# Gated sum of two linear-attention branches on one core: the key-value burst moved behind the first denominators, W' among later queries, 1/den by Ln and Exp

## The chip, the cores and the metric

The kernel runs on one core of one Trainium2 chip. The metric is the device time of one execution in microseconds (us). All executions used below ran in the fast state (granted TensorE clock 1.0), with one exception that is named where it comes up. PE is TensorE (PEld is its weight loads), DVE is VectorE, ACT is ScalarE, POOL is GpSimd, SP is SyncE. PSUM is the memory that the matmuls write to; in this kernel a PSUM bank stays taken until another engine has read it out (a *drain*). The experiments ran in three sets on three chips, each set with the kernel before in the same rounds, so across sets the ratios to it are compared and not the times.

## The reference, cut to what matters

```python
# two branches X in (A, B), each with its own wqkv and wo; S = 2048, D = 640, 32 heads of 20
qkv = x @ wqkv
phi = lambda t: jnp.where(t > 0, t + 1, jnp.exp(t)) + 1e-6
pq, pk = phi(q), phi(k)
kv  = einsum("bhsd,bhse->bhde", pk, v)
z   = einsum("bhsd->bhd", pk)
num = einsum("bhqd,bhde->bhqe", pq, kv)
den = einsum("bhqd,bhd->bhq", pq, z) + 1e-6
o   = (num / den) @ wo
out = g * o_A + (1 - g) * o_B        # g = sigmoid(sum(x * gate_w))
```

The kernel never forms `v`. For each branch it forms G = phi(k)ᵀx, then per head kv = G·Wv, and then W' = kv·Wo, so that the output is (phi(q)/den)·W'.

## The kernel before

A small list scheduler in the kernel's Python orders all operations. Each operation has a *planned* duration, and the scheduler also hands out the eight PSUM banks. The order and the banks are then fixed in the program.

The phases on PE are: keys of both branches, G of A, G of B, queries in four blocks of 512 rows (each block has five "query units" per branch), then the totals (`final`), 128 rows at a time. The key-value step `m_unit` (110 small matmuls for both branches, over two column groups of the array), its masks on DVE and the W' pairs sit at different places for the two branches. The small matmuls and the denominators are *column-tiled*: they use 64 and 32 columns of PE's array (`128*64` and `128*32` in the traces).

```python
def m_unit(X):                                   # 55 small matmuls into one bank, then three masks
    ...
    for q0, q1, g, w in ((0, 5, 0, 12), (0, 5, 1, 12), (5, 6, last, 8)):
        def mask(e, ...):
            return e.tensor_tensor(
                out=MB[p0 : p0 + n, q0:q1, 60 * g : 60 * g + n].rearrange("p q (i k) -> p q k i", k=NC),
                in0=PS[p0 : p0 + n, tile.banks[0], ...].rearrange("p (q k i) -> p q k i", k=NC, i=w),
                in1=m.unsqueeze(1).to_broadcast([n, q1 - q0, NC, w]), op=ALU.mult)
        sch.op("DVE", mask, _dve_ns(n * (q1 - q0)), ...)      # planned: 380 ns for 60x300

g_unit("B", 0); g_unit("B", 1); m_unit("A")      # A: inside the G phase of B
g_unit("B", 2)
for q in (0, 1): wp_unit("A", q)                 # W' pair: 2 matmuls into a pair of banks, one drain
...
queries(0)
m_unit("B")                                      # B: between query blocks 0 and 1,
queries(1)                                       #    W' pairs of B among the queries of block 1
wp_store("B"); wp_rows("B")                      # W' through DRAM, back as WPB
d01 = dens(0)                                    # denominators of blocks 0 and 1
scale_q(0, d01, 2)                               # ACT copies den, DVE reciprocal, factors through DRAM,
queries(2); queries(3)                           #    then DVE multiplies the queries
...
# ---- scale_q (cut) ----
e.activation(DN, PS[den], ACT.Identity, bias=EP)            # ACT
e.reciprocal(RC, DN)                                        # DVE
# ---- final (cut): for each piece of columns: A total, ACT drain times g; B total, DVE blend ----
```

## Time and profile before

| | before |
|---|---|
| time, median of the first 6 executions | 190.67 us (190.61 to 190.99) |
| span of the profiled execution | 189.5 us |
| PE / DVE / ACT busy | 98% / 68% / 40% |
| PE waiting, all at the start | 1.4 us |
| first query matmul | 94.98 us |

The first two parts of the page give the busy time of each engine and, below, its busy tenths in 40 slices of the span. The fourth part gives the chain of work that ended last; a q behind an engine's name is its queue or sequencer, and "issue" is time in which nothing visible was waited for.

```profile
PE 185.9 (98%) x1289; PEld 124.0 (65%) x1289; DVE 129.8 (68%) x275; ACT 76.5 (40%) x129; POOL 8.2 (4%) x14
...
PE   7999999999999999999999999999999999999995
...
DVE  1398998999600009996179997898999959933324
...
PE 94%; DMA 3%; SPq 1%; issue 0%; ACT 0%; DVE 0%; DVEq 0%; ACTq 0%
```

PE has no gap after its start, and the chain is PE for 94% of the span. Nothing that other engines do counts until it makes PE wait.

The groups by shape show busy us, mean ns of one instruction, and the idle time of the engine before them:

```profile
L793 DVE RECIPROCAL RC<-DN 128x256 bf16<-128x256 f32 x4 | 7.0, 1746 | 0.1
L647 DVE TENSOR_TENSOR MB<-ps,CB 60x300 bf16<-60x300 f32 x4 | 4.1, 1032 | 0.1
L787 ACT ACTIVATE DN<-ps,EP 128x256 f32<-128x256 f32 x4 | 1.9, 474 | 1.2 <-PE ps L383 1.1
```

The timeline (start us, duration us, what) of the small bursts and of the end:

```profile
105.86 1.13 PE L383 MATMUL ps<-GTB,WVB 128*64 128x60 bf16 x55
106.92 3.43 PE L383 MATMUL ps<-XT,WQA 128*128 128x512 bf16 x15
...
116.97 0.44 PE L383 MATMUL ps<-WOB,MB 124*120 124x320 bf16 x2
117.24 2.32 PE L383 MATMUL ps<-XT,WQB 128*128 128x512 bf16 x10
119.40 2.32 PE L383 MATMUL ps<-XT,WQA 128*128 128x512 bf16 x10
...
122.53 0.38 PE L383 MATMUL ps<-FE,ZBDB 128*32 128x512 bf16 x2
122.85 3.44 PE L383 MATMUL ps<-XT,WQA 128*128 128x512 bf16 x15
...
186.75 0.51 PE L383 MATMUL ps<-WPB,FE 128*128 128x160 bf16 x5
...
187.01 0.39 ACT L859 ACTIVATE TS<-ps,GA 128x160 f32<-128x160 f32 x1 [0.36 <-PE ps L383]
187.51 0.38 DVE L865 SCALAR_TENSOR_TENSOR OL<-ps,GA,TS 128x160 bf16<-128x160 f32 x1 [0.37 <-ACT TS L859]
```

Query matmuls start 0.216 us apart. After the denominators the next one comes 0.32 us later, so leaving a column-tiled burst costs 0.1 us. PE's last matmul ends at 187.26 (186.75 + 0.51), and the last blend at 187.89 (187.51 + 0.38).

### The profile page before, as it was taken

What the parts mean: (1) busy time and instruction counts of PE and PEld (TensorE: products, weight loads), DVE (VectorE), ACT (ScalarE), POOL (GpSimd) and SP (SyncE); (2) the same over time, 40 slices, a digit from 0 to 9 for tenths busy, and PEclk for the clock granted to TensorE, in tenths of its full rate; (3) what the DMA queues carried; (4) which work ended last, traced back from release to release, by engine and by line L of the source; (5) the groups of instructions that cost most, each with busy time, mean ns of one, the idle gap of its engine ahead of it and who ended that gap; (6) DMA issues with size and microseconds to landing.
All of it is one profiled execution on the core that took longest, in us unless ns stands there. A gap on an engine that the chain in (4) does not pass through costs nothing.

```text
span 189.5 us, 3208 instructions
## 1 busy us (share of the span) xinstructions
PE 185.9 (98%) x1289; PEld 124.0 (65%) x1289; DVE 129.8 (68%) x275; ACT 76.5 (40%) x129; POOL 8.2 (4%) x14
## 2 busy tenths in 40 slices
PE   7999999999999999999999999999999999999995
PEld 2555555555788888888855666455556677777774
DVE  1398998999600009996179997898999959933324
ACT  2265656565311122103255478565553422332232
POOL 8900000000000000000000000000000000000000
DMA  5999699991011111112143004675000173221212
GB/s 189 298 243 177 211 388 364 337 231 33 0 35 38 35 35 38 35 35 38 35 95 102 5 22 173 166 224 170 0 0 3 44 226 92 86 89 35 73 69 69
DMA packets 31936, 21.49 MB, mean 113 GB/s; under 512 B 16818, under 2 KB 31666, under 8 KB 31922
## 3 DMA queue, kind: packets, MB, share of 16 engines
q1 hardware_dynamic: 31490, 20.80, 39.5%
q10 hardware_dynamic: 432, 0.49, 0.8%
q8 instruction: 10, 0.16, 0.4%
q14 instruction: 4, 0.03, 0.1%
HBM read 12.05 MB, written 5.31 MB: 92 GB/s over the span
## 4 chain that ended last, share of the span: by engine, by line
PE 94%; DMA 3%; SPq 1%; issue 0%; ACT 0%; DVE 0%; DVEq 0%; ACTq 0%
PE ps L383 94%; DMA WK<-in_B_wqkv_dram 3%; SPq L372 1%; ACT TS L859 0%; DVE OL L865 0%; DVEq L276 0%; ACTq L276 0%
## 5 line engine op out<-in xcount | busy, mean ns | idle before, releaser
L383 PE MATMUL ps<-WK,XT 128*128 128x512 bf16 (+2 forms) x250 | 44.0, 337 | 0.5 <-DMA WK<-in_A_wqkv_dram 0.2
L383 PE MATMUL ps<-XN,FE 128*128 128x320 bf16 x320 | 44.3, 300 | 0.0
L383 PEld LDWEIGHTS ps<-XN,FE 128*128 128x128 bf16 x320 | 37.5, 118 | 5.9
L383 PEld LDWEIGHTS ps<-WK,XT 128*128 128x128 bf16 x250 | 24.1, 98 | 20.0 <-DMA WK<-in_A_wqkv_dram 0.5
L743 ACT ACTIVATE EK<-ps 128x512 bf16<-128x512 f32 x40 | 23.9, 597 | 18.5 <-PE ps L383 16.9
L563 ACT ACTIVATE EK<-ps 128x512 bf16<-128x512 f32 (+1 forms) x42 | 21.4, 526 | 16.2 <-PE ps L383 16.2
L752 DVE SCALAR_TENSOR_TENSOR FE<-ps,EK 128x512 bf16<-128x512 f32 x40 | 26.8, 688 | 0.7
L859 ACT ACTIVATE TS<-ps,GA 128x640 f32<-128x640 f32 (+2 forms) x18 | 13.2, 734 | 29.5 <-PE ps L383 29.5
L383 PE MATMUL ps<-WPB,FE 128*128 128x320 bf16 (+1 forms) x165 | 24.7, 295 | 0.0
L383 PE MATMUL ps<-WPA,FE 128*128 128x320 bf16 (+1 forms) x165 | 24.7, 295 | 0.0
L573 DVE SCALAR_TENSOR_TENSOR FE<-ps,EK 128x512 bf16<-128x512 f32 (+1 forms) x42 | 23.9, 596 | 0.5
L865 DVE SCALAR_TENSOR_TENSOR OS<-ps,GA,TS 128x640 bf16<-128x640 f32 x15 | 13.0, 869 | 14.7 <-PE ps L383 14.7
L383 PE MATMUL ps<-XT,WQA 128*128 128x512 bf16 x100 | 22.8, 380 | 0.0
L383 PE MATMUL ps<-XT,WQB 128*128 128x512 bf16 x100 | 22.7, 379 | 0.0
L600 ACT ACTIVATE GS<-ps 128x640 bf16<-128x640 f32 x10 | 7.0, 704 | 37.0 <-PE ps L383 37.0
L383 PEld LDWEIGHTS ps<-WPA,FE 128*128 128x128 bf16 x165 | 15.9, 98 | 6.1
L383 PEld LDWEIGHTS ps<-WPB,FE 128*128 128x128 bf16 x165 | 15.8, 98 | 6.2 <-ACT TS L859 0.4
L383 PEld LDWEIGHTS ps<-XT,WQB 128*128 128x128 bf16 x100 | 11.7, 117 | 9.1
L383 PEld LDWEIGHTS ps<-XT,WQA 128*128 128x128 bf16 x100 | 11.6, 118 | 9.4 <-issue 0.4
L705 DVE SCALAR_TENSOR_TENSOR GP<-XN,GWB 128x640 bf16<-128x640 bf16 x16 | 13.3, 829 | 4.1 <-PE ps L383 3.6
L811 DVE TENSOR_TENSOR FE<-FE,RX 128x1280 bf16<-128x1280 bf16 (+1 forms) x20 | 12.6, 685 | 1.6 <-DMA RX<-factor 1.6
L567 DVE TENSOR_SCALAR EK<-EK 128x512 bf16<-128x512 bf16 (+1 forms) x42 | 11.4, 272 | 3.1
(52 smaller groups left out, 80.3 us busy)
## 6 DMA issues: line engine op xcount, KB each, us to landing
out_dram<-OS SPq DMA_DIRECT2D x15, 160.0 KB, 1.8
XN<-in_A_x_dram SPq DMA_DIRECT2D x3, 640.0 KB, 8.1
factor<-RC SPq DMA_DIRECT2D x4, 256.0 KB, 2.6
RX<-factor SPq DMA_DIRECT2D x4, 256.0 KB, 3.2
WVA<-in_A_wqkv_dram SPq DMA_DIRECT2D x1, 800.0 KB, 10.4
WQA<-in_A_wqkv_dram SPq DMA_DIRECT2D x1, 800.0 KB, 11.9
WVB<-in_B_wqkv_dram SPq DMA_DIRECT2D x1, 800.0 KB, 11.2
WQB<-in_B_wqkv_dram SPq DMA_DIRECT2D x1, 800.0 KB, 12.5
```

The source lines that it names most:

```text
L372: ins = e.dma_start(dst() if callable(dst) else dst, src() if callable(src) else src, transpose=transpose)
L383: ins = pe.matmul(o, l, r, start=a, stop=z, tile_position=tp, skip_group_check=True)
L563: "ACT", lambda e, ps=ps, ek=ek: e.activation(ek(), ps(), ACT.Exp), _act_ns(n), reads=[(tile,)], writes=[(es,)],
L567: "DVE", lambda e, ek=ek: e.tensor_scalar(ek(), ek(), 1.0, EPS, op0=ALU.min, op1=ALU.add), _dve_ns(n, 4),
L573: return e.scalar_tensor_tensor(out=out, in0=two(ps()), scalar=0.0, in1=two(ek()), op0=ALU.max, op1=ALU.add)
L600: "ACT", lambda e: e.activation(GS[:, k, :].rearrange("p (h f) -> p h f", f=HALF), pair(tile, HALF), ACT.Copy),
L705: lambda e, t=t: e.scalar_tensor_tensor(out=GP[:, :], in0=XN[:, t, 0:D], scalar=1.0, in1=GWB[:, :], op0=ALU.mult, op1=ALU.mult, accum_out= ...
L743: "ACT", lambda e: e.activation(ek(), PS[:, tile.banks[0], :], ACT.Exp), _act_ns(512), reads=[(tile,)],
L752: lambda e: e.scalar_tensor_tensor(out=dst, in0=PS[:, tile.banks[0], :], scalar=0.0, in1=ek(), op0=ALU.max, op1=ALU.add),
L811: return e.tensor_tensor(out=v, in0=v, in1=RX[:, xs.slot, 512 * x + w * j : 512 * x + w * j + w].unsqueeze(1).to_broadcast([128, NC, w]), ...
L859: "ACT", lambda e, acc=acc, t_ap=t_ap: e.activation(t_ap(), acc(), ACT.Copy, scale=GA[:, 0, t : t + 1]),
L865: lambda e, acc=acc, t_ap=t_ap, o_ap=o_ap: e.scalar_tensor_tensor(out=o_ap(), in0=acc(), scalar=GA[:, 1, t : t + 1], in1=t_ap(), op0=ALU.m ...
```

## The change

The intent was to gather the key-value matmuls of both branches in one burst right behind the first denominators, which are column-tiled too. The W' pairs then fall among the queries of blocks 2 and 3. The reciprocals leave DVE for ACT, so that DVE has room for the masks. In the last tile, the A total of the next piece runs ahead of the B total of the current one, so that its drain is done earlier.

```diff
+        sch.op("ACT", lambda e: e.preload_act_table_set("natural_log_exp_and_others"), 1300, name="table")
...
-        def m_unit(X):
+        def m_both(after):
+            tiles = [_Tile(1), _Tile(1)]                     # 110 matmuls, two banks, one semaphore at the end
...                                                           # six masks; each waits for the one before
-            if X == "A" and q % 2 == 0:                      # W' drains: three on DVE, eight on ACT
-                sch.op("DVE", lambda e: e.tensor_copy(dst, src()), ...)
-            else:
-                sch.op("ACT", lambda e: e.activation(dst, src(), ACT.Copy), ...)
+            sch.op("ACT", lambda e: e.activation(ws(u)..., PS[...], ACT.Copy), ...)      # all on ACT
...
-                lambda e: e.activation(DN[...], PS[...], ACT.Identity, bias=EP[:, 0:1])
+                lambda e: e.activation(DN[...], PS[...], ACT.Ln, bias=EP[:, 0:1])
-            sch.op("DVE", rec, 1740, reads=[(ds,)], writes=[(ds,)], name="rc%d" % b)
+            sch.op("ACT", lambda e: e.activation(RC[...], DN[...], ACT.Exp, scale=-1.0), ...)
...
+            for i, (lo, hi) in enumerate(parts):             # last tile: A0, A1, B0, A2, B1, B2
+                if i == 0:
+                    total(0, lo, hi)
+                if i + 1 < len(parts):
+                    total(0, *parts[i + 1])
+                total(1, lo, hi)
...
         queries(0)
-        m_unit("B")
         queries(1)
-        wp_store("B")
-        wp_rows("B")
-        d01 = dens(0)
+        d01, den = dens(0)
+        m_both(den)
+        queries(2)                                           # with W' pairs among queries(2) and queries(3)
         scale_q(0, d01, 2)
-        queries(2)
         queries(3)
```

The matmuls of PE are the same in number and shape before and after.

More of the change, by code (lines that the diff above doesn't have):

```diff
@@ L27 @@
 HALF = 320
-WPLAG = 2
+WPLAG = 3
 XW = 672
@@ L324, in bass_gated_mix__linear_attn_block__linear_attn_block__prompt_kernel @@
         W5 = sb("W5", [128, D])
-        MB = sb("MB", [128, 6, 120])
+        MB = sb("MB", [128, 11, 120])
         WS = sb("WS", [120, 6, D])
@@ L406, in bass_gated_mix__linear_attn_block__linear_attn_block__prompt_kernel @@
         sch.op("POOL", lambda e: e.memset(W5[:, :], 0.0), 500, writes=[("W5", X) for X in XS], name="w5z")
-        sch.op("POOL", lambda e: e.memset(MB[:, :, :], 0.0), 700, writes=[("M", q) for q in range(6)], name="mz")
+        sch.op("POOL", lambda e: e.memset(MB[:, :, :], 0.0), 700, writes=[("M", q) for q in range(11)], name="mz")
         def load_x(eng, t):
@@ L620, in zbd, with step, mask @@
             )
-        def m_unit(X):
-            tile = _Tile(1)
-            last = XS.index(X)
-            def steps():
-                r = []
-                for q in range(6):
-                    w = 12 if q < 5 else 8
-                    for j in range(NC):
-                        for g in (0, 1) if q < 5 else (last,):
-                            at = D * j + 120 * q + 60 * g * (q < 5)
-                            r.append((
-                                PS[64 * g : 64 * g + 64, tile.banks[0], 60 * q : 60 * q + NC * w], WV[X][:, at : at + 64],
-                                GT[X][:, j, :, 24 * q + 12 * g * (q < 5) : 24 * q + 12 * g * (q < 5) + w], j == 0, j == NC - 1, (0, 64 * g),
-                            ))
-                return r
-            mms("m%s" % X, steps, [("GT", X, k) for k in range(NC)] + [("WV", X), ("WVP", X)], [(tile,)], 25 * 75 + 400)
-            for q0, q1, g, w in ((0, 5, 0, 12), (0, 5, 1, 12), (5, 6, last, 8)):
+        def m_both(after):
+            tiles = [_Tile(1), _Tile(1)]
+            def step(x, q, g, j):
+                w, lo = (12, 12 * g) if q < 5 else (8, 0)
+                at = D * j + 120 * q + DH * lo // 4
+                return (
+                    PS[64 * g : 64 * g + 64, tiles[x].banks[0], 60 * q : 60 * q + NC * w], WV[XS[x]][:, at : at + 64],
+                    GT[XS[x]][:, j, :, 24 * q + lo : 24 * q + lo + w], j == 0, j == NC - 1, (0, 64 * g),
+                )
+            def steps():
+                r = [step(x, q, g, j) for x in (0, 1) for q in range(5) for j in range(NC) for g in (0, 1)]
+                return r + [step(x, 5, x, j) for j in range(NC) for x in (0, 1)]
+            mms(
+                "m", steps, [("GT", X, k) for X in XS for k in range(NC)] + [("WV", X) for X in XS] + [("WVP", X) for X in XS],
+                [(t,) for t in tiles], 110 * 38 + 240, after=after,
+            )
+            for x, q0, q1, g, w in ((0, 0, 5, 0, 12), (0, 0, 5, 1, 12), (0, 5, 6, 0, 8), (1, 5, 6, 1, 8), (1, 0, 5, 0, 12), (1, 0, 5, 1, 12)):
                 n = DH * (w // 4)
-                def mask(e, q0=q0, q1=q1, g=g, w=w, n=n):
+                o0 = 10 if q0 == 5 else 5 * x
+                def mask(e, x=x, q0=q0, q1=q1, o0=o0, g=g, w=w, n=n):
                     p0 = 64 * g
@@ L647, in mask @@
                     return e.tensor_tensor(
-                        out=MB[p0 : p0 + n, q0:q1, 60 * g : 60 * g + n].rearrange("p q (i k) -> p q k i", k=NC),
-                        in0=PS[p0 : p0 + n, tile.banks[0], 60 * q0 : 60 * q0 + n * (q1 - q0)].rearrange("p (q k i) -> p q k i", k=NC, i=w),
+                        out=MB[p0 : p0 + n, o0 : o0 + q1 - q0, 60 * g : 60 * g + n].rearrange("p q (i k) -> p q k i", k=NC),
+                        in0=PS[p0 : p0 + n, tiles[x].banks[0], 60 * q0 : 60 * q0 + n * (q1 - q0)].rearrange(
+                            "p (q k i) -> p q k i", k=NC, i=w
+                        ),
                         in1=m.unsqueeze(1).to_broadcast([n, q1 - q0, NC, w]), op=ALU.mult,
@@ L653, in m_unit, with ws, wp_unit @@
                 sch.op(
-                    "DVE", mask, _dve_ns(n * (q1 - q0)), reads=[(tile,), ("CB",)], writes=[("M", q) for q in range(q0, q1)],
-                    name="mm%s" % X,
-                )
-        def wp_unit(X, q):
+                    "DVE", mask, _dve_ns(n * (q1 - q0)), reads=[(tiles[x],), ("CB",)], writes=[("M", q) for q in range(o0, o0 + q1 - q0)],
+                    name="mm%d" % x,
+                )
+        def ws(u):
+            return GS[0:120, u, :] if u < 5 else WS[:, u - 5, :]
+        def wp_unit(u):
             tile = _Tile(2)
-            w = W5 if q == 5 else WO[X][:, q, :]
+            X = XS[min(u // 5, 1)]
+            w = W5 if u == 10 else WO[X][:, u % 5, :]
             def steps():
                 return [
-                    (PS[0:120, tile.banks[h], 0:HALF], MB[0:124, q, :], w[0:124, HALF * h : HALF * h + HALF], True, True, None)
+                    (PS[0:120, tile.banks[h], 0:HALF], MB[0:124, u, :], w[0:124, HALF * h : HALF * h + HALF], True, True, None)
                     for h in (0, 1)
@@ L669, in wp_unit @@
             mms(
-                "wp%s%d" % (X, q), steps, [("M", q)] + [("W5", Y) for Y in XS if q == 5] + [("WO", X, g) for g in (0, 1) if q < 5],
+                "wp%d" % u, steps, [("M", u)] + [("W5", Y) for Y in XS if u == 10] + [("WO", X, g) for g in (0, 1) if u < 10],
                 [(tile,)], D + 60,
             )
-            dst = WS[:, q, :].rearrange("p (h f) -> p h f", f=HALF)
-            def src():
-                return PS[0:120, tile.banks[0] : tile.banks[1] + 1, 0:HALF]
-            name = "wpe%s%d" % (X, q)
-            if X == "A" and q % 2 == 0:
-                sch.op("DVE", lambda e: e.tensor_copy(dst, src()), _dve_ns(D), reads=[(tile,)], writes=[("WS", q)], name=name)
-            else:
-                sch.op("ACT", lambda e: e.activation(dst, src(), ACT.Copy), _act_ns(D), reads=[(tile,)], writes=[("WS", q)], name=name)
+            sch.op(
+                "ACT",
+                lambda e: e.activation(
+                    ws(u).rearrange("p (h f) -> p h f", f=HALF), PS[0:120, tile.banks[0] : tile.banks[1] + 1, 0:HALF], ACT.Copy
+                ),
+                _act_ns(D), reads=[(tile,)], writes=[("WS", u)] + [("GS", u)] * (u < 5), name="wpe%d" % u,
+            )
         def wp_store(X):
+            u0 = 5 * XS.index(X)
             dma(
-                "SP", "ws" + X, WD[X].ap()[0:600, :].rearrange("(q p) f -> p q f", p=120), WS[:, 0:5, :], reads=[("WS", q) for q in range(5)],
-                writes=[("WD", X, 0)], us=2.0,
+                "SP", "ws" + X, WD[X].ap()[0:600, :].rearrange("(q p) f -> p q f", p=120), (GS[0:120, :, :] if X == "A" else WS[:, 0:5, :]),
+                reads=[("WS", u) for u in range(u0, u0 + 5)], writes=[("WD", X, 0)], us=2.0,
             )
@@ L693, in wp_rows @@
             p0 = 60 * XS.index(X)
-            dma("SP", "ws5" + X, nat[600:D, :], WS[p0 : p0 + 40, 5, :], reads=[("WS", 5)], writes=[("WD", X, 5)], us=0.2)
+            dma("SP", "ws5" + X, nat[600:D, :], WS[p0 : p0 + 40, 5, :], reads=[("WS", 10)], writes=[("WD", X, 5)], us=0.2)
             dma(
@@ L773, in den @@
                 return r
-            mms(
+            o = mms(
                 "den%d" % b0, den, [("ZBD", X) for X in XS] + [("PQ", X, k, b) for X in XS for k in range(NC) for b in (b0, b0 + 1)],
@@ L778, in dens @@
             )
-            return dtile
+            return dtile, o
         def scale_q(b, dtile, pieces):
@@ L786, in scale_q @@
                 "ACT",
-                lambda e: e.activation(DN[:, ds.slot, :], PS[:, dtile.banks[0], lo : lo + 256], ACT.Identity, bias=EP[:, 0:1]), _act_ns(256),
+                lambda e: e.activation(DN[:, ds.slot, :], PS[:, dtile.banks[0], lo : lo + 256], ACT.Ln, bias=EP[:, 0:1]), _act_ns(256),
                 reads=[(dtile,), ("EP",)], writes=[(ds,)], name="dn%d" % b,
             )
-            def rec(e):
-                with nc.allow_low_precision(reason="the factor is a bf16 matmul operand"):
-                    return e.reciprocal(RC[:, ds.slot, :], DN[:, ds.slot, :])
-            sch.op("DVE", rec, 1740, reads=[(ds,)], writes=[(ds,)], name="rc%d" % b)
+            sch.op(
+                "ACT", lambda e: e.activation(RC[:, ds.slot, :], DN[:, ds.slot, :], ACT.Exp, scale=-1.0), _act_ns(256, False), reads=[(ds,)],
+                writes=[(ds,)], name="rc%d" % b,
+            )
             rep = FD[b].ap()
@@ L826, in final, with total, steps, acc @@
             row = out[0, 128 * t : 128 * t + 128, :]
-            for lo, hi in parts:
+            got = {}
+            def total(x, lo, hi):
                 n = 1 if hi - lo <= 512 else 2
                 w = (hi - lo) // n
-                ts = _Tile(1, ring["ts"])
-                def o_ap(lo=lo, hi=hi, w=w):
+                X = XS[x]
+                tile = _Tile(n)
+                ts = got.setdefault(lo, _Tile(1, ring["ts"]))
+                def steps():
+                    return [
+                        (PS[:, tile.banks[h], 0:w], PQ[X][:, k, 128 * t : 128 * t + 128],
+                         WP[X][:, k, lo + w * h : lo + w * h + w], k == 0, k == NC - 1, None)
+                        for k in range(NC) for h in range(n)
+                    ]
+                def acc():
+                    return PS[:, tile.banks[0] : tile.banks[0] + n, 0:w]
+                def o_ap():
@@ L833, in o_ap, with t_ap @@
                     v = OL[:, lo:hi] if last else OS[:, os.slot, lo:hi]
                     return v.rearrange("p (h f) -> p h f", f=w)
-                def t_ap(ts=ts, hi=hi, lo=lo, w=w):
+                def t_ap():
                     return TS[:, ts.slot, 0 : hi - lo].rearrange("p (h f) -> p h f", f=w)
-                okey = ("OL", lo) if last else (os,)
-                for x, X in enumerate(XS):
-                    tile = _Tile(n)
-                    def steps(X=X, tile=tile, lo=lo, w=w, n=n):
-                        return [
-                            (PS[:, tile.banks[h], 0:w], PQ[X][:, k, 128 * t : 128 * t + 128],
-                             WP[X][:, k, lo + w * h : lo + w * h + w], k == 0, k == NC - 1, None)
-                            for k in range(NC) for h in range(n)
-                        ]
-                    def acc(tile=tile, n=n, w=w):
-                        b0 = tile.banks[0]
-                        return PS[:, b0 : b0 + n, 0:w]
-                    mms(
-                        "f%s%d" % (X, t), steps, [("PQS", X, t)] + [("WP", X, k) for k in range(NC)], [(tile,)], 5 * n * (w + 6),
-                    )
-                    if x == 0:
-                        sch.op(
-                            "ACT", lambda e, acc=acc, t_ap=t_ap: e.activation(t_ap(), acc(), ACT.Copy, scale=GA[:, 0, t : t + 1]),
-                            _act_ns(hi - lo), reads=[(tile,), ("GA",)], writes=[(ts,)], name="fa%d" % t,
-                        )
-                    else:
-                        sch.op(
-                            "DVE",
-                            lambda e, acc=acc, t_ap=t_ap, o_ap=o_ap: e.scalar_tensor_tensor(
-                                out=o_ap(), in0=acc(), scalar=GA[:, 1, t : t + 1], in1=t_ap(), op0=ALU.mult, op1=ALU.add
-                            ),
-                            _dve_ns(hi - lo), reads=[(tile,), (ts,), ("GA",)], writes=[okey], name="fb%d" % t,
-                        )
@@ new lines, in total @@
+                mms("f%s%d" % (X, t), steps, [("PQS", X, t)] + [("WP", X, k) for k in range(NC)], [(tile,)], 5 * n * (w + 6))
+                if x == 0:
+                    sch.op(
+                        "ACT", lambda e: e.activation(t_ap(), acc(), ACT.Copy, scale=GA[:, 0, t : t + 1]), _act_ns(hi - lo),
+                        reads=[(tile,), ("GA",)], writes=[(ts,)], name="fa%d" % t,
+                    )
+                    return
+                sch.op(
+                    "DVE",
+                    lambda e: e.scalar_tensor_tensor(
+                        out=o_ap(), in0=acc(), scalar=GA[:, 1, t : t + 1], in1=t_ap(), op0=ALU.mult, op1=ALU.add
+                    ),
+                    _dve_ns(hi - lo), reads=[(tile,), (ts,), ("GA",)], writes=[("OL", lo) if last else (os,)], name="fb%d" % t,
+                )
@@ L873, in final @@
                         "SP", "out%d_%d" % (t, lo), row[:, p0:hi],
-                        (lambda p0=p0, hi=hi: OL[:, p0:hi]) if last else (lambda: OS[:, os.slot, :]),
+                        (lambda: OL[:, p0:hi]) if last else (lambda: OS[:, os.slot, :]),
                         reads=[("OL", c) for c, _ in parts if p0 <= c < hi] if last else [(os,)], us=0.4,
                     ))
+            for i, (lo, hi) in enumerate(parts):
[4 more added lines that the diff above has]
+                total(1, lo, hi)
         kt = {(X, t): _Tile(2) for X in XS for t in (0, 1)}
@@ L901, in bass_gated_mix__linear_attn_block__linear_attn_block__prompt_kernel @@
         gates()
-        g_unit("B", 0)
-        g_unit("B", 1)
-        m_unit("A")
-        g_unit("B", 2)
-        for q in (0, 1):
-            wp_unit("A", q)
-        g_unit("B", 3)
-        for q in (2, 3):
-            wp_unit("A", q)
-        g_unit("B", 4)
-        wp_unit("A", 4)
-        wp_store("A")
+        for k in range(NC):
+            g_unit("B", k)
         zbd("B")
+        order = [0, 1, 2, 3, 4, 10, 5, 6, 7, 8, 9]
         def queries(b):
@@ L918, in queries @@
                     q_unit(X, b, k)
-                    q = 5 * (X == "B") + k - WPLAG
-                    if b == 1 and 0 <= q < 6:
-                        wp_unit("B", (q - 1) % 6)
-                        if q == 0:
+                    i = 10 * (b - 2) + 5 * (X == "B") + k - WPLAG
+                    if 0 <= i < 11:
+                        wp_unit(order[i])
+                        if i == 5:
+                            wp_store("A")
                             wp_rows("A")
+                        if i == 10:
+                            wp_store("B")
+                            wp_rows("B")
         def finals(b):
@@ L932, in bass_gated_mix__linear_attn_block__linear_attn_block__prompt_kernel @@
         queries(0)
-        m_unit("B")
         queries(1)
-        wp_store("B")
-        wp_rows("B")
-        d01 = dens(0)
+        d01, den = dens(0)
+        m_both(den)
+        queries(2)
         scale_q(0, d01, 2)
-        queries(2)
         queries(3)
         scale_q(1, d01, 2)
-        d23 = dens(2)
+        d23, _ = dens(2)
         finals(0)
```

## The prediction

> **What bounds it now.** TensorE. The page gives PE busy 98% of a 189.5 us span, and the chain of waits is 94% PE: one unbroken run of matmuls from 9.05 to 186.93 us. The waits of PE sum to 1.4 us, all at the start. ScalarE is 40% busy, VectorE 68%. After the last matmul come one ScalarE drain (0.39 us), then the last VectorE blend (0.38 us), then the output transfer. So there is little to win; only PE work, PE stalls and the tail count.
>
> **What does not count.** The four reciprocals (1.75 us each on VectorE) go; ScalarE gets four Exp of 128x256 instead ([...]the Ln should cost what the 0.47 us Identity did). [...]one table load (1.28 us in this trace) should remain. No PE instruction waited for those reciprocals, so about 7 us of saved VectorE time are worth nothing by themselves. PE's matmuls are the same in number and shape.
>
> **What helps.**
> 1. Tail: the last piece's branch-A total now runs before the previous piece's branch-B total, so its ScalarE drain leaves the end: about -0.43 us (drain plus handover; timeline of the end).
> 2. The column-tiled bursts. [...]some 0.1 us extra at entry and again at exit of a burst (after the first denominators 0.32 us to the next matmul instead of 0.22). Four bursts become two: about -0.3 us. The 110 small matmuls still take 19 ns each.
>
> **What hurts.** Masks and W' units now fall among the queries that also carry the scaling multiplies.
> 3. By the scheduled order, the first W' unit waits for the second mask of branch A, and query unit B0 of block 2 takes the PSUM bank that the last of six masks frees. A mask takes 1.02 us and serial ones start 1.07 apart; the last should end about 4.4 us after the burst, while PE gets there after 3.8. Stall about 0.2 + 0.65 us.
> 4. W' pairs occupy four banks, so a query unit reuses the bank of the fourth before it. VectorE needs about 1.55 us per unit with a multiply (0.2 + 0.74 + 0.6), PE 1.36 (five matmuls 1.08, W' pair 0.28). The backlog stays just inside; 0 to 0.7 us more if those three cost 1.65.
> 5. W' of B is needed by the first branch-B total. Before, from the end of the last W' pair (117.24) to the landing of WPB (127.86) took 10.6 us. Afterwards PE has six query units (6.5), two A totals (2.7) and the denominators (1.3) to hide it: 10.5. Stall about 0.3 us, 0 to 1.
>
> Sum: -0.43 - 0.3 + 0.85 + 0.1 + 0.3 = about +0.5, but the stalls are the uncertain part and could vanish. I predict 190.9 us, 189.8 to 192.0 in 8 of 10; faster by over 2%: 0.02, within 2%: 0.96, slower by over 2%: 0.02.
>
> **What would show it.** Waits of PE: MATMUL after the burst waiting for the masks (0.2 and 0.65 us), waits for VectorE query results among the W' units, a wait for the WPB load before the first B total. Timeline: den and burst adjacent with no gap, the A drain of the last piece done before its B matmuls end. ScalarE: one table load. VectorE busy 7 us less for reciprocals.
>
> **What would make it wrong.** The simple gains (1, 2) without stalls: 190.0. A slower VectorE backlog, ScalarE unable to hold exp plus W' drain (1.3 us in 1.36), or slower WPB transfers: 192 or more. A different exp cost in the other table set would show in every phase.

That the bursts cost something at entry and exit rests on the 0.1 us of the trace of before alone.

## The result, and the profile after

The changed kernel took 191.81 us, median of 6 executions (191.19 to 192.25), against 190.67 us. The ratio is 1.0053, with a 95% interval of 1.0034 to 1.0072. All ratios here are the mean time of one kernel's fast runs over that of the other's of the same rounds, so not quite the ratio of the medians quoted. It is slower by about 1 us, inside the 2% that counts as the same, and inside the predicted range.

The page of the changed kernel, parts 1, 2 and 4:

```profile
PE 186.1 (97%) x1289; PEld 123.6 (65%) x1289; DVE 123.0 (64%) x268; ACT 79.7 (42%) x136; POOL 8.7 (5%) x14
...
PE   8899999999999999999999999989999999999995
...
PE 91%; DMA 3%; DVE 3%; SPq 1%; issue 0%; DVEq 0%
```

DVE is 6.8 us less busy, and yet it has entered the chain. The slice late in the span where PE drops from 9 to 8 (124.1 to 128.9 us) is the place. The groups that answer to those of before:

```profile
L651 DVE TENSOR_TENSOR MB<-ps,CB 60x300 bf16<-60x300 f32 x4 | 4.1, 1026 | 1.4 <-PE ps L383 1.3
...
L795 ACT ACTIVATE DN<-ps,EP 128x256 f32<-128x256 f32 x4 | 1.9, 466 | 1.0 <-PE ps L383 1.0
L800 ACT ACTIVATE RC<-DN 128x256 bf16<-128x256 f32 x4 | 1.7, 417 | 0.1
```

The Ln costs what the Identity did, and the Exp 0.42 us. One table load remains (1283 ns in both traces). The timeline of PE around the burst:

```profile
117.65 0.38 PE L383 MATMUL ps<-FE,ZBDB 128*32 128x512 bf16 x2
117.96 0.98 PE L383 MATMUL ps<-GTA,WVA 128*64 128x60 bf16 x50
118.77 0.96 PE L383 MATMUL ps<-GTB,WVB 128*64 128x60 bf16 x50
...
119.81 2.35 PE L383 MATMUL ps<-XT,WQA 128*128 128x512 bf16 x10
122.16 0.45 PE L383 MATMUL ps<-WOA,MB 124*120 124x320 bf16 x2
122.45 1.24 PE L383 MATMUL ps<-XT,WQA 128*128 128x512 bf16 x5
123.53 0.44 PE L383 MATMUL ps<-WOA,MB 124*120 124x320 bf16 x2
124.92 1.27 PE L383 MATMUL ps<-XT,WQB 128*128 128x512 bf16 x5 [0.95 <-DVE MB L651]
```

Undisturbed, ten query matmuls take 2.16 us and a W' pair 0.27 to 0.28 us from start to start (117.24 to 119.40 and 116.97 to 117.24 in the timeline of before). The first W' pair is therefore 0.19 us late (122.16 - 119.81 = 2.35), and query unit B0 of block 2 is 1.12 us late (124.92 - 123.53 = 1.39). The chain in order of time names what it waited for:

```profile
9.56 110.34 PE ps L383 x784
...
119.92 1.03 DVE MB L651
...
120.98 1.04 DVE MB L651
...
122.05 0.27 DVE MB L651
...
122.34 0.30 DVE MB L651
...
122.67 1.02 DVE MB L651
123.69 0.13 DVE EK L755
...
123.84 1.03 DVE MB L651
...
124.92 63.52 PE ps L383 x438
188.44 0.03 issue
...
188.54 0.30 DVE OL L869
...
188.88 0.38 DVE OL L869
```

The six masks run one after another from the end of the burst, and the last frees the PSUM bank in which unit B0 is to be written. At the end, no ACT drain stands behind PE any more, but two blends follow each other instead.

Where the time went, from the two profiled executions (minus = gained):

| part | us | how it is read |
|---|---|---|
| start, up to the first query matmul | +0.49 | 92.93 against 94.98 less the 2.54 us of key-value and W' work that stood before it |
| small bursts | -0.47 | before 1.06 + 1.06 + 1.19 us and three entries of 0.1; after 1.19 + 1.85 and one entry |
| first W' pair waits for masks | +0.19 | timeline above |
| query unit B0 waits for the last mask | +1.12 | timeline above |
| a later query unit among the W' pairs | +0.16 | 0.43 instead of 0.27 us behind its W' pair |
| end of PE to end of the last blend | -0.14 | 0.49 instead of 0.63 us |
| sum | +1.35 | spans 190.9 - 189.5 = 1.4 |

The start does not belong to the change. Over the profiles, with the same correction for the kernels that do that work early, the first query matmul came anywhere between 92.1 and 92.9 us: mean 92.57 in the four kernels with the start of before, 92.55 in the ten with that of the changed one. (In all profiles but these two the record of the first query matmul is missing, 24 records in its group and not 25; it is set 0.216 us before the first one recorded.) Without the start, the change loses about 0.86 us by the rows of the table. Taken whole, the time from the first query matmul to the end, called the *start-free time* below, is 97.99 us against 97.10 (the latter with the 2.54 us added): 0.89 us. Each such figure comes from one profile; a repeat differed by 0.02 us.

### The profile page after: what moved, and what is told of

Same layout as the page of the kernel before. It is cut to its first block, busy times and chain, and to the rows that moved or that the text cites. A ratio compares the mean times of both kernels' runs of the same rounds, so it can differ in the third digit from the quotient of the medians.

```text
span 190.9 us, 3207 instructions
## 1 busy us (share of the span) xinstructions
PE 186.1 (97%) x1289; PEld 123.6 (65%) x1289; DVE 123.0 (64%) x268; ACT 79.7 (42%) x136; POOL 8.7 (5%) x14
## 4 chain that ended last, share of the span: by engine, by line
PE 91%; DMA 3%; DVE 3%; SPq 1%; issue 0%; DVEq 0%
PE ps L383 91%; DMA WK<-in_B_wqkv_dram 3%; DVE MB L651 2%; SPq L372 1%; DVE OL L869 0%; DVE EK L755 0%; DVEq L276 0%
## 5 line engine op out<-in xcount | busy, mean ns | idle before, releaser
L383 PE MATMUL ps<-XN,FE 128*128 128x320 bf16 x320 | 43.8, 300 | 0.0
L760 DVE SCALAR_TENSOR_TENSOR FE<-ps,EK 128x512 bf16<-128x512 f32 x40 | 27.5, 690 | 1.0
L383 PE MATMUL ps<-XT,WQA 128*128 128x512 bf16 x100 | 23.3, 380 | 0.0
```

What stands on the lines that cost most here:

```text
L383: ins = pe.matmul(o, l, r, start=a, stop=z, tile_position=tp, skip_group_check=True)
L760: lambda e: e.scalar_tensor_tensor(out=dst, in0=PS[:, tile.banks[0], :], scalar=0.0, in1=ek(), op0=ALU.max, op1=ALU.add),
```

## The experiments

The theory at this point was: serial masks hold a PSUM bank, and PE loses 1.3 us to them. Rivals were: the start, too much DVE work in general, and the new ACT work or table set.

### The changed kernel again

> The changed kernel once more, unaltered, with five rounds. Theory (PE stalls behind the serial masks, 1.46 us, against 0.5 us of savings): again 0.4 to 0.6% above the kernel before, and in the trace the same stalls to within 0.1 us: 0.2 us before the first W' pair, 1.1 us before query unit B0 of block 2. Rival (the loss is in the start, where the wait for the WK loads was 0.5 us longer in the one profile that we have): the start differs from run to run, the median comes near 190.9, and the stalls among the queries explain only part.

Measured: 191.9 us, ratio 1.0063 (1.0048 to 1.0079). The stalls were there again in its trace: 0.9 us counted as a wait at unit B0, which started 1.38 us behind its W' pair. The first query matmul came at 92.62 us, 0.31 us earlier than in the first profile, and the start-free time was 97.97 us, against 97.99. The loss is in the program, not in the start.

### Masks that do not wait for each other

```diff
                 sch.op("DVE", mask, ...)
+                mine = sch.ops[-1]
+                for d in mine.deps:
+                    if d.eng == "DVE":
+                        mine.deps[d] = False
```

> The six masks no longer wait for each other (they write disjoint partitions or columns and run on one engine in order); every engine's order and every PSUM bank stay as in the changed kernel. Theory: masks start some 0.77 us apart instead of 1.07, the last one ends about 1.3 us earlier, both stalls (0.2 and 1.1 us) go: about 190.4 us, 1.3 us below the changed kernel and 0.3 below the one before. Rival (VectorE has too much work in that stretch, whatever the waits, or the loss is elsewhere): the stall only moves to a later query unit, and the time stays within 0.3 us of the changed kernel.

Measured: 191.67 us, ratio 1.0050 (1.0033 to 1.0067), against 1.0063 for the changed kernel in the same rounds. That is a quarter of a microsecond at best, not 1.3, and the intervals overlap; the start-free time is 97.93 us, against 97.97 in the repeat. DVE's first five masks, merged on one line of the timeline:

```profile
119.10 3.71 DVE L651 TENSOR_TENSOR MB<-ps,CB 60x300 bf16<-60x300 f32 x5 [1.34 <-PE ps L383]
```

PE's list of waits (total us, count, longest us) still has the masks:

```profile
PE ps L383 <- DVE MB L651: 0.9, 1, 0.9
```

In the repeat of the changed kernel the same five took 3.77 us. So this part of the theory fell: the waits between the masks cost next to nothing. I had read a 0.77 us distance in the trace of before as the cost of a mask that waits for nothing, but there the next operation was of another kind. The kind is not what decides, though: in the next section two masks with no wait between them start 0.79 us apart. Those two start at the same partition (64), while neighbours among the six start at partitions 0 and 64 in turn. In the trace of before, too, the next operation started 0.77 us behind a mask of partition 0 (80.75 to 81.52) and 1.07 us behind one of partition 64 (82.47 to 83.54), the next one starting at partition 0 both times. That the start partitions decide fits these traces, but it was not tested.

By this pair of traces (3.77 and 3.71 us), the semaphores between the five masks add 0.06 us at most. And an operation can start before the one ahead of it has ended: 0.79 us lie between the two starts, and the first of these masks took 1.02 us.

### One more mask, and a control

```diff
+                    if (x, g, q0) == (1, 1, 0):          # before the last mask, into a scratch tile
+                        one(SCR[p0 : p0 + n, :, 60 * g : 60 * g + n])
```

> One more mask operation of the same shape (into a scratch tile) just before the last of the six; orders and banks unchanged. Theory: the bank that query unit B0 of block 2 needs comes free 0.8 to 1.0 us later, and PE loses all of it: about +0.9 us over the changed kernel, the stall there 1.9 to 2.1 us. Rival (the masks' end is not what PE waits for, or the wait is made good later): within 0.3 us of the changed kernel.

Measured: 192.39 us (192.01 to 193.08), ratio 1.0093. PE's wait grew from 0.95 to 1.81 us:

```profile
123.04 0.44 PE L384 MATMUL ps<-WOA,MB 124*120 124x320 bf16 x2
125.29 1.27 PE L384 MATMUL ps<-XT,WQB 128*128 128x512 bf16 x5 [1.81 <-DVE MB L653]
```

On DVE, the added mask and the last of the six:

```profile
123.35 1.02 DVE L653 TENSOR_TENSOR SCR<-ps,CB 60x300 bf16<-60x300 f32 x1
124.14 1.10 DVE L653 TENSOR_TENSOR MB<-ps,CB 60x300 bf16<-60x300 f32 x1
```

The time rose by 0.6 us over the repeat of the changed kernel (mean 192.47 against 191.89), somewhat less than the stall. The spread of these four runs is 1 us, so the 0.3 us between them is not resolved by the times. The profiles resolve it: the start-free time is 98.87 us against 97.97, so PE lost all of the 0.9 us.

The control adds one blend of 0.88 us for tile 11 into a scratch tile:

```diff
+                    if t == 11:
+                        one(SCR[:, :].rearrange("p (h f) -> p h f", f=HALF))
```

> As a control, one more VectorE operation of 0.88 us among the totals (tile 11, into a scratch tile), where VectorE waits 1.8 us per tile for PE. Theory: no change, within 0.2 us of the changed kernel. Rival (any VectorE work now costs time): about +0.8 us.

Measured: 191.76 us, ratio 1.0056 (the changed kernel in the same rounds 1.0063), and a start-free time of 97.99 us against 97.97: nothing. DVE work costs time just behind the burst, and none among the totals.

### The same masks, walked in the other order

If the waits are not the cost, the mask's own 1.02 us is. It handles only 300 elements per partition, but its output steps five elements (10 bytes) at a time.

```diff
-  out=MB[...].rearrange("p q (i k) -> p q k i", k=NC),
-  in0=PS[...].rearrange("p (q k i) -> p q k i", k=NC, i=w),
-  in1=m.unsqueeze(1).to_broadcast([n, q1 - q0, NC, w])
+  out=MB[...].rearrange("p q (i k) -> p q i k", k=NC),
+  in0=PS[...].rearrange("p (q k i) -> p q i k", k=NC, i=w),
+  in1=m.rearrange("p k i -> p i k").unsqueeze(1).to_broadcast([n, q1 - q0, w, NC])
```

> The chain of waits among the masks was not what made them slow (without it they still started 1.06 us apart), so the new theory is that the mask's own 1.02 us for 60x300 is the cost, 3.4 ns per element of a partition, and that its scattered output (stride 5 elements) is why. Here the same masks walk the output contiguously and read PSUM with a stride instead; result, order, waits and banks unchanged. Theory: the mask falls to 0.4 to 0.7 us, the last one ends 1.5 us or more earlier, both stalls (0.2 and 1.1 us) go: about 190.4 us. Rival (the stride is merely moved to the reading side, or the cost is in the four-dimensional pattern): the mask stays near 1.0 us and the time near 191.8.

Measured: 190.38 us, ratio 0.9973 (0.9948 to 0.9998) to the kernel before, with the right result. The mask's group:

```profile
L651 DVE TENSOR_TENSOR MB<-ps,CB 60x300 bf16<-60x300 f32 x4 | 2.8, 690 | 1.4 <-PE ps L383 1.3
```

PE's list of waits no longer has an entry for the masks, and unit B0 (second line) starts 0.28 us behind its W' pair:

```profile
123.03 0.44 PE L383 MATMUL ps<-WOA,MB 124*120 124x320 bf16 x2
123.31 1.24 PE L383 MATMUL ps<-XT,WQB 128*128 128x512 bf16 x5
```

From first to last mask the starts span 2.87 us (119.60 to 122.47) instead of 3.92. Both mask stalls are gone, and with them the 1.4 us between this kernel and the changed one (the start-free time is 96.60 us against 97.97): the loss was the masks' time. A mask of 300 elements per partition takes 0.69 us with the contiguous output and 1.02 us with the stepped one, although PSUM and the mask are now read with a stride. Shown is that the walking order alone takes a third off; by what mechanism was not shown.

### The same masks, with their true duration in the plan

```diff
-  "DVE", mask, _dve_ns(n * (q1 - q0)), ...
+  "DVE", mask, (1020 if q0 == 0 else 260), ...
```

> The scheduler gets the measured time of the masks (1020 and 260 ns instead of 380 and 110), nothing else. It then puts query unit A4 before the first W' pair, gives query unit B0 another bank, and spreads the masks among the query operations. Theory (the stall comes from a wrong duration in the plan): the two mask stalls go, some 0.5 us of stalls for W' drains come instead; about 191.0, 0.8 us below the changed kernel. Rival (too little PSUM, whatever the plan): the stall returns elsewhere in full, 191.6 or more.

Measured: 190.38 us, ratio 0.9976 (0.9954 to 0.9999). The masks are as slow as ever (1033 ns), but no PE wait on them is left; the weight loads wait 0.6 us in two places for W' drains. So the stall was not the only possible fate of slow masks. A plan that knew they take 1.02 us, not 0.38, avoids it. It gained more than the 0.8 us expected (a start-free time of 96.64 us, 1.3 less than the repeat of the changed kernel).

Both together:

> Both cures together: the quicker masks, and their measured time (690 and 220 ns) in the scheduler's plan. Theory: with the masks at 0.69 us no PE wait on them was left, so the plan has nothing more to win: 190.3, within 0.2 us of the quicker masks alone (0.27% below the kernel before). Rival (two independent gains): about 189.8.

Measured: 190.39 us, ratio 0.9974 (0.9951 to 0.9996). The two cures remove the same stall and do not add. A small new wait also appeared: PE waited 0.3 us for the load of W' of branch B, and the start-free time is 96.82 us, against 96.60 with the quicker masks alone. These three kernels beat both the kernel before and the changed one, by 0.25% over the former. The intervals only just exclude zero: a real difference, but a small one.

### Only the last tile's order

```diff
   # kernel before, with the changed kernel's final() and nothing else
```

> The kernel before, with only the order of the last tile's totals changed. By the changed kernel's trace the gain is 0.14 us, not the 0.43 predicted, because the removed drain had already overlapped PE's B total, and the last two blends now follow each other. Theory: the time from the end of PE's last matmul to the end of the last blend falls from 0.63 to 0.49 us; total -0.1 to -0.2 us. Rival (as predicted first): -0.4 us.

Measured: 190.72 us against 190.89, ratio 0.9987 (0.9971 to 1.0003): not resolved as a time. The interval is -0.55 to +0.06 us, so it holds the rival's 0.4 us as well; the trace decides. PE's last matmul ends at 187.33 (186.47 + 0.86, second line below), the last blend at 187.82. That is 0.49 us, as in the changed kernel, and the start-free time is 96.96 us against 97.10: the 0.14 us expected.

```profile
186.40 1.42 DVE L862 SCALAR_TENSOR_TENSOR OL<-ps,GA,TS 128x320 bf16<-128x320 f32 x3 [0.79 <-PE ps L383]
...
186.47 0.86 PE L383 MATMUL ps<-WPB,FE 128*128 128x160 bf16 x10
```

### Only Ln and Exp, twice

> The kernel before, with only the reciprocal moved to ScalarE as Ln and Exp. Theory: nothing waits for the reciprocals, so within 0.2 us of the kernel before; VectorE 7 us less busy, one table load. Rival (the other table set or the extra ScalarE work costs time, and so is a part of the loss): 0.5 us or more slower.

```diff
   # kernel before, plus the table preload, Ln and Exp on ScalarE; everything else as before
```

Measured: 191.83 us, ratio 1.0048 (1.0029 to 1.0067): slower, which the theory had not expected. But no ACT operation grew (exp of 128x512: 597 ns in both). The waits:

```profile
PE ps L383 <- DVE FE L754: 0.7, 1, 0.7
...
DVE FE L812 <- DMA RX<-factor: 2.9, 2, 1.5
```

Without the 1.74 us reciprocals in its plan, the scheduler put the multiplies earlier on DVE than their factors arrive. DVE stood still for 2.9 us (1.6 before), the last queries came out late, and the second denominators waited for them. The start-free time grew by 0.87 us (97.97 against 97.10). To test that, only the planned transfer times were mended:

```diff
-  writes=[("FD", b)], us=0.6      # factor write
+  writes=[("FD", b)], us=2.6
-  writes=[(xs,)], us=0.6          # factor read
+  writes=[(xs,)], us=1.4
```

> The kernel before with Ln and Exp on ScalarE was 0.9 us slower, where none was expected. In its trace no ScalarE operation grew; VectorE stood 2.9 us waiting for the factor loads (1.6 before) because the plan, freed of the reciprocals, put the multiplies too early, and the second denominators then waited 0.9 us. Here the plan gets the measured transfer times of the factors (about 4.6 and 2.9 us instead of 2.6 and 2.6). Theory (the order, not the Exp, costs): back to within 0.3 us of the kernel before. Rival (Ln and Exp or their table set cost time): still 0.6 us or more slower.

Measured: 191.15 us against 190.78, ratio 1.0006 (0.9975 to 1.0037), and no DVE wait for the factors. The interval reaches from -0.5 to +0.7 us, so the times alone do not exclude the rival; the start-free time does, with 97.11 us against 97.10. So Ln, Exp and their table set cost nothing measurable by themselves; the order that followed from them did.

### The changed kernel with its reciprocals back on DVE

```diff
-  e.activation(DN, ..., ACT.Ln, ...);       ACT: e.activation(RC, DN, ACT.Exp, scale=-1.0)
+  e.activation(DN, ..., ACT.Identity, ...); DVE: e.reciprocal(RC, DN)
```

> The changed kernel with the reciprocals back on VectorE (1.75 us each). The plan puts two of them among the masks. Theory (VectorE's time just behind the burst is what PE waits for, so here the Exp on ScalarE does earn something): PE stalls of 2 us or more, 0.5 to 1.0 us slower than the changed kernel, about 192.5. Rival (the reciprocals are free wherever they stand, as in the kernel before): the same as the changed kernel.

Measured: 195.34 us (fast runs 195.15 to 195.34), ratio 1.0228 (1.0198 to 1.0259). The direction is right and the size far off: 3.2 to 3.3 us more than the changed kernel by the ratios, not 0.5 to 1.0. (Whether it is over 2% slower than the kernel before stays unclear, as the interval begins below.) Its profile fell in the one slow execution of four (198.58 us, clock 0.983), so only the waits and the clock are read from it, and no duration behind the first of them in time, the second line:

```profile
PE ps L383 <- DMA WPB<-wrowsB: 2.2, 1, 2.2
PE ps L383 <- DVE FE L760: 1.9, 1, 1.9
```

A W' pair waited 1.9 us for a query operation that stood behind the reciprocals and masks on DVE. The other wait, for W' of branch B, I had not foreseen. That one may have another length in the fast runs; how the 3.3 us divide is open. Behind both waits the granted clock of this execution was lower: 0.66 from 129 to 134 us, behind the wait of 1.9 us, and 6 tenths on the page in the slice from 152.8 to 157.8 us, behind the one of 2.2 us. In the kernel with one more mask the clock was 1.0 in spite of a PE wait of 1.8 us, and so it was in the other three executions of this one. It was not followed up.

Under this plan, then, the Exp on ACT is what makes a burst at this place affordable, although the same reciprocals were free in the kernel before. The reciprocals changed the planned order too, and a plan with the masks' true durations was not tried with them.

### The slack of W' of branch B

```diff
-WPLAG = 3
+WPLAG = 5        # on the kernel with the quicker masks: every W' pair two query units later
```

> The kernel with the quicker masks, and every W' pair two query units later. This measures the slack of the W' load of branch B, which was predicted to stall PE for 0.3 us and just did not. From the last W' pair to the first B total PE now has four query units, three A totals and the denominators, 9.7 us, where the drain, the store and the load take 10.4 to 10.6. Theory: PE waits 0.7 to 0.9 us for WPB, and the time is 0.6 to 1.0 us above that of the quicker masks alone. Rival (the load has slack): no wait, same time.

Measured: 191.56 us (191.24 to 192.44), ratio 1.0041 (1.0009 to 1.0073). PE waits for the load:

```profile
PE ps L383 <- DMA WPB<-wrowsB: 0.7, 1, 0.7
```

The wait has the size expected; the time is about 1.3 us above that of the quicker masks (1.0041 against 0.9973, each relative to before), a little more than expected. These two come from different sets, and the four runs spread over 1.2 us; by the start-free time it is 0.89 us (97.49 against 96.60). So the load really stands at the edge, as the 0.3 us wait in the kernel with both cures also says. In the changed kernel the weight loads before the first B total waited 0.4 us for it, hidden behind the denominators, and PE not at all.

## Why the prediction was right or wrong

The range, the class and the direction were right: 190.9 predicted, 191.81 measured, 189.8 to 192.0 stated. The mechanism was right too: small gains in the bursts and at the end, outweighed by PE waiting for the masks behind the burst. Point by point:

- **"So there is little to win".** Right. Saving 6.8 us of DVE time won nothing of itself. Taken alone it even cost 0.9 us, through the order that the planner then chose.
- **Step 1, the tail, "about -0.43 us": mis-sized.** It measured 0.14. Of the removed ACT drain (0.39 us) only the last 0.14 us stood behind PE's last matmul (187.26 to 187.40), with 0.11 us of handover; the rest had run under PE's B total. In its place now stand 0.07 us of the blend before the last (188.77 to 188.84) and 0.04 us between the blends.
- **Step 2, the bursts, "about -0.3 us".** It measured -0.47. Of six changes of mode three remain, each 0.1 us: the step from the 32-column denominators to the 64-column burst costs one as well (0.31 us to the next matmul, 117.65 to 117.96), so the boundary inside the joined burst is not free. The other 0.17 us come from quicker matmuls: 110 took 1.85 us to the next query (before 2 x 1.06). Less 0.1 us for each exit, that is about 16 ns each instead of 17.5. Before, five 40-column matmuls of a branch stood in a row on one column group; afterwards the two branches alternate. That this is the reason is argued, not tested.
- **Step 3, the masks, "Stall about 0.2 + 0.65 us": the term most off.** It measured 0.19 + 1.12. I let the last mask end 4.4 us after the burst, counting some masks as overlapping at 0.77 us. The six did not overlap one another: the last one ended 5.06 us after it (124.87 - 119.81), and removing the waits between them shortened the first five by 0.06 us. The wait itself, and which bank it was for, were right: one more mask lengthened it by 0.86 us, and quicker masks removed it.
- **Step 4, the backlog, 0 to 0.7 us.** A unit with a multiply took DVE 1.54 us (from its first operation to that of the next, 127.96 to 129.50), and one later unit was 0.16 us late. Right.
- **Step 5, W' of B, "Stall about 0.3 us, 0 to 1".** PE waited 0.0 us; the slack of about zero was confirmed by moving the pairs two units later.
- **The sum.** The parts came to +0.5, and I then predicted only +0.2, because "the stalls are the uncertain part and could vanish". They grew instead. The steps measured +0.86 in sum, the start-free time +0.87 to +0.89, and the runs about +1.0 to +1.2; the 0.1 to 0.3 us between them stays open. That the sum came this close is partly luck: the tail, the masks and the backlog missed by +0.8 us together, the bursts and W' of B by -0.5.

## What to carry to other kernels

Where one engine has no gaps, ask of every moved operation whose PSUM bank it holds and until when, and cost it with its measured duration: here 300 elements took 1.02 us where the planner had 0.38, and either true figure in the plan or a contiguous output removed the whole stall. Taking work off an engine that is not on the chain can cost time (0.87 us here) when a planner, with optimistic transfer times, reorders around the hole. Before crediting a shorter tail, check what already ran under the last matmuls.
